# Projections as two 64-row tiles of the array side by side, with kv's sums a chunk later

## The chip, the cores and the metric

The kernel runs on one core of a Trainium2 chip. A core has five engines with queues of their own: TensorE (matmuls, PE in the profile, its weight loads PEld), VectorE (DVE), ScalarE (ACT), GpSimd (POOL) and SyncE (SP), which here only issues DMAs. Matmuls read SBUF and write PSUM, eight banks of 128 partitions by 512 float32; VectorE and ScalarE read PSUM out. The metric is the device time of one execution in microseconds.

## What is computed

Two branches of a block on the same x (2048 x 512), mixed by a gate. All inputs are float32.

```python
def _A_ref(x, wqkv, w_phi, wo):                      # 32 heads of 16
    qkv = (x @ wqkv) ...                             # q, k, v per head
    pq = einsum("bhsd,hdf->bhsf", q, w_phi)
    pk = einsum("bhsd,hdf->bhsf", k, w_phi)
    phi_q = concat([softmax(pq), softmax(-pq)])      # 32 features per head
    phi_k = concat([softmax(pk), softmax(-pk)])
    kv = einsum("bhsf,bhsd->bhfd", phi_k, v)
    z  = einsum("bhsf->bhf", phi_k)
    num = einsum("bhqf,bhfd->bhqd", phi_q, kv)
    den = einsum("bhqf,bhf->bhq", phi_q, z)[..., None] + 1e-6
    return (num / den) ... @ wo
def _B_ref(x, w1, b1, w2):                           # 512 -> 1376 -> 512
    h = x @ w1 + b1
    return (h * tanh(softplus(h))) @ w2
g = sigmoid((x * gate_w).sum(-1, keepdims=True))
out = g * _A_ref(x) + (1 - g) * _B_ref(x)
```

kv and z are sums over all 2048 rows, so every k and v must be there before the first num.

## The kernel before

The matrix products keep float32 accuracy by splitting each operand into a high and a low part in the type float32r, whose matmul is quick: a product is hi x hi + hi x lo + lo x hi. w_phi is multiplied into wk and wq at the start (fuse, L213 and fuse_tiles, L219), so k and q come out of the projection as pk and pq.

The first phase, ("A", c), goes over x in eight chunks of 256 rows (c = 0 to 7), each of two row tiles of 128 (t = 0, 1). For each chunk and row tile there are three projections, k, v and q (proj, L230), each one PSUM tile of 128 x 512 that sums 12 matmuls: 4 slices of the 512 contraction rows (128 each) for each of the three products. The stationary operand is x, 128 rows by the 128 rows of the row tile; the moving one is the weight, 128 x 512. Then, for each row tile:

- k (feat_ops, L250): VectorE takes the maximum and the minimum per head (mx, mn), subtracts (d0, d1; L263 and L265) into a tile E of 128 x 1024 in SBUF, ScalarE takes the exponential (E), VectorE sums per head (S), takes the reciprocal (rS) and scales E (ml, L280). GpSimd adds E to zacc (z, L318). E lives in one of four buffers until the sums of kv have read it.
- v: ScalarE copies it to SBUF (ve).
- q: ScalarE copies it to SBUF (qe) and SyncE stores it to DRAM (st), from where the second phase loads it again (lq).
- kv (L320): 16 small matmuls per row tile add E and v into one PSUM tile that is kept over all chunks.

PSUM is handed out under three tags (L116): a with three buffers, dn with four, kv with one. k and q tiles take a, v tiles take dn (the very first v takes kv). A new tile waits until the readers of the one that had its buffer are done.

The second phase, ("B", b), goes over four blocks of 512 rows. It multiplies x by w1 in 11 slices of 128 columns (up), applies Mish, multiplies by w2 (dn), does for q what was done for k, and combines: num, wo and the gate. x is loaded and split again for it: xbh on ScalarE (XH), xbl on VectorE (XL, L403), which take over the buffers of wk. The weights w1 and w2 are loaded piece by piece and split during the first phase (ldw, wh, wl).

The order of work is written out by hand: strings of step names (FIRST to BLOCK, L39 to L86), which run (L199) reads word by word. Each word calls the function recorded under that name for the chunk; a trailing ' means the chunk before, a trailing + the first block of the second phase (or the next block). All instructions are pinned to this order on their engine, so the strings set the queue of every engine. Before, chunks 1 to 5 use ODD and EVEN in turn, 6 uses NEXT and 7 uses LAST:

```python
ODD = """
    k0 xh mx0 mn0 d00 d10 xl ldx k1 wh0 E0 wl0 ldw0 mx1 mn1 d01 d11 v0 wh1 E1 S0 rS0 ml0 z0 ve0 v1 wl1 ldw1
    S1 rS1 ml1 z1 ve1 q0 qe0 st0 q1 qe1 st1 kv' kv
"""
```

Here k0 is the projection k of row tile 0. The kv sums stand behind every second chunk, for that chunk and the one before; for chunks 6 and 7 they are in LAST.

Of the kernel before, what the change touches and what calls it, by code (L numbers as in the profile page):

```python
# [15 lines left out]
P = 128  # L16
# [20 lines left out]


FIRST = """  # L39
    fq v0 fh0 fh1 fh2 fh3 fl0 fl1 mx0 mn0 d00 d10 fl2 fl3 xh xl ldx ve0 E0 mx1 mn1 d01 d11 v1 ve1 E1  # L40
    S0 rS0 ml0 z0 ldw0 ldw1 S1 rS1 ml1 z1 q0 qe0 st0 q1 qe1 st1
"""
EVEN = """
    k0 xh mx0 mn0 d00 d10 xl ldx k1 wh0 E0 wl0 ldw0 mx1 mn1 d01 d11 v0 wh1 E1 S0 rS0 ml0 z0 ve0 v1 wl1 ldw1
    S1 rS1 ml1 z1 ve1 q0 qe0 st0 q1 qe1 st1
"""
ODD = """
    k0 xh mx0 mn0 d00 d10 xl ldx k1 wh0 E0 wl0 ldw0 mx1 mn1 d01 d11 v0 wh1 E1 S0 rS0 ml0 z0 ve0 v1 wl1 ldw1
    S1 rS1 ml1 z1 ve1 q0 qe0 st0 q1 qe1 st1 kv' kv
"""  # L50
NEXT = """
    lq0+ k0 xh mx0 mn0 d00 d10 xl ldx k1 wh0 E0 wl0 ldw0 mx1 mn1 d01 d11 wh1 E1 S0 rS0 ml0 z0 v0 ve0 wl1 ldw1
    S1 rS1 ml1 z1 v1 ve1 q0 mx0+ mn0+ d00+ d10+ qe0 st0 q1 qe1 st1 E0+ lq1+
"""
LAST = """
    k0 mx0 mn0 d00 d10 k1 E0 XH0 kv' mx1 mn1 d01 d11 E1 v0 S0 rS0 ml0 z0 ve0 ldo XH1 mx1+ mn1+ d01+ d11+ E1+
    S1 rS1 ml1 z1 XL0 XL1 v1 ve1 lq2+ q0 WH0 qe0 st0 q1 WH1 zh qe1 st1 zl kv S0+ rS0+ km
"""

BLOCK0 = """
    up0 mi0 hi0 lo0 gr lq3 S1 rS1 mx2 mn2 d02 d12 up1 @z mi1 hi1 lo1 T0 D0 m0 de0 rd0 sc0 es0 tr0 up2 mi2 hi2 lo2 WL0 dn0
# [7 lines left out]
BLOCK1 = """  # L71
# [7 lines left out]
BLOCK = """  # L79
# [10 lines left out]
def tile_gated_mix(ctx: ExitStack, tc: tile.TileContext, xT, wv, wkT, wqT, bd, w1a, w1b, b1, w2a, w2b, wo, out):  # L90
# [4 lines left out]

    nm = [0]
    pin = tc.keep_in_program_order
    V, G_, A_, Sy = nc.vector, nc.gpsimd, nc.scalar, nc.sync

    def mm(*a, **k):  # L100
        return pin(nc.tensor.matmul(*a, **k))  # L101
# [5 lines left out]
    def k8(name, tag, dt=F32R):  # L107
        return T([P, 2048], dt, tag, 1, name)
# [4 lines left out]
    def k2(name, tag, dt=F32):  # L113
        return T([P, 512], dt, tag, {"pq": 3, "io": 4, "hl": 8}[tag], name)

    def psum(name, tag, bufs={"a": 3, "dn": 4, "kv": 1}):  # L116
        nm[0] += 1
        return pp.tile([P, 512], F32, name=f"{name}_{nm[0]}", tag=tag, bufs=bufs[tag])

    def act(out_, in_, fn=AF.Copy, **k):  # L120
        return pin(A_.activation(out_, in_, fn, **k))  # L121
# [48 lines left out]
    ps = psum("warm", "dn")  # L170
# [35 lines left out]
    wkh, wkl, wvh, wvl, wqh, wql = [
        kt(k8(n, t), 512) for n, t in (("wkh", "xbh"), ("wkl", "xbl"), ("wvh", "woh"), ("wvl", "wol"), ("wqh", "tt"), ("wql", "eT"))]
    xs, Es, vs, psA = {}, {}, {}, {}
# [18 lines left out]
                        mm(acc[r // 64][c : c + 64, o : o + 64], staged[r : r + 64, k, G, c : c + 64], bds[r : r + 64, G, r : r + 64], start=True, stop=True, skip_group_check=True)  # L227
        return acc

    def proj(x, t, wh, wl, tag):  # L230
        ps = psum("proj", tag)
        xh, xl = x
        sl = slice(t * P, (t + 1) * P)
        n = 0
        for a, w in ((xh, wh), (xh, wl), (xl, wh)):
            for k in range(KT):
                mm(ps, a[k // 2][:, k % 2, sl], w[:, k, :], start=(n == 0), stop=(n == 3 * KT - 1))
                n += 1
        return ps
# [10 lines left out]
    def feat_ops(key, t, src, d):  # L250

        n = str(t)

        def red(name, op):
            d[name] = T([P, H], F32, name, 2, name)
            pin(V.tensor_reduce(d[name], hv(src()), axis=AX.X, op=op))  # L256

        def dd(a):
            if "E" not in d:
                d["E"] = k4("E", "E")  # L260
            E = hv(d["E"][:, a * 512 : (a + 1) * 512])
            if a == 0:
                pin(V.tensor_sub(E, hv(src()), d["mx"][:, :, None].to_broadcast([P, H, DH])))  # L263
            else:
                pin(V.tensor_sub(E, d["mn"][:, :, None].to_broadcast([P, H, DH]), hv(src())))  # L265

        def ss():
            d["S"] = T([P, 2 * H], F32, "Sm", 2, "Sm")
            pin(V.tensor_reduce(d["S"], hv(d["E"][:, :]), axis=AX.X, op=ALU.add))  # L269
# [12 lines left out]
    def a_ops(c):  # L282
        key = ("A", c)
        P_ = psA[c] = {}
        for t in range(2):
            d = {}
            Es[c, t] = d

            def k_(t=t):
                P_["k", t] = proj(xs[c], t, wkh, wkl, "a")  # L290

            def v_(t=t):
                P_["v", t] = proj(xs[c], t, wvh, wvl, "dn" if c or t else "kv")

            def q_(t=t):
                P_["q", t] = proj(xs[c], t, wqh, wql, "a")
# [12 lines left out]

            at(key, f"k{t}", k_)  # L310
            at(key, f"v{t}", v_)
            at(key, f"q{t}", q_)
            at(key, f"ve{t}", ve)
            at(key, f"qe{t}", qe)
            at(key, f"st{t}", st)
            feat_ops(key, t, lambda t=t: P_["k", t][:, :], d)
            at(key, f"ml{t}", lambda d=d: scale_by(d, V))
            at(key, f"z{t}", lambda d=d: pin(G_.tensor_add(zacc, zacc, d["E"])))  # L318

        def kv():  # L320
# [115 lines left out]
    B = {}  # L436
# [266 lines left out]

    for t in range(2):
        psA[0]["k", t] = pk[t]
        del steps[("A", 0), f"k{t}"]

    run(FIRST, ("A", 0))
    for c in range(1, NCH):
        run((EVEN, ODD)[c % 2] if c < NCH - 2 else NEXT if c < NCH - 1 else LAST, ("A", c), ("A", c - 1), ("B", 0))  # L710
    for b in range(NB):
        run((BLOCK0, BLOCK1, BLOCK, BLOCK)[b], ("B", b), ("B", b - 1), ("B", b + 1))
    assert not steps, list(steps)


# [58 lines left out]
```

## Time and profile before

| | us |
|---|---|
| median of 3 runs | 457.28 (456.52 to 458.05) |
| span of the profiled execution | 455.6 |
| TensorE busy | 445.6 |
| VectorE busy | 306.8 |
| ScalarE busy | 195.0 |
| GpSimd busy | 161.4 |

The span is that of one execution from its first to its last instruction, taken by the hardware profiler; what the runs take beyond it is 1.7 us by the median. In rows of the profile, "L101 PE MATMUL proj<-wkh,xh 128\*128 128x512" is a matmul recorded at line 101 (a helper that all matmuls go through), which writes proj from wkh and xh, with a tile of the array of 128 rows by 128 columns and an output of 128 x 512. The number after x is how many; then come busy microseconds and the mean length of one in ns. Matmuls overlap in the pipeline, so the time from one start to the next, not the length of one, is what a matmul costs. "[1.51 <-DVE xbl L403]" is idle time before an instruction and what ended it. SBUF and PSUM types of four bytes are both shown as f32.

### The profile page before, as it was taken

Reading aid. Unit: us, or ns where it says so; the run is one execution under the profiler, and the core shown is the slowest. Engines: PE = TensorE matmul, PEld = TensorE weight load, DVE = VectorE, ACT = ScalarE, POOL = GpSimd, SP = SyncE. Lnnn points to the kernel's source line nnn. Section 1 sums busy time; section 2 is a strip of 40 time slices with the busy share of each in tenths; the row PEclk is TensorE's granted clock in tenths of the full one; section 3 lists DMA queues with packets and bytes.
Section 4 is the critical chain, followed back from the end, with each engine's and each line's share of the span. In section 5 each row is a group of like instructions: output and inputs, shape, how many; then the busy total and the mean of one; then the engine's idle time right before and its main releaser. Section 6 shows DMA issues by size and latency. Waiting matters only on the chain.

```text
span 455.6 us, 6980 instructions
## 1 busy us (share of the span) xinstructions
PE 445.6 (98%) x2772; PEld 363.4 (80%) x2772; DVE 306.8 (67%) x402; ACT 195.0 (43%) x265; POOL 161.4 (35%) x102
## 2 busy tenths in 40 slices
PE   7999999999999899999899999999999999999996
PEld 6888888888888678878687887887887888787885
DVE  2599459369399999799987985666967629611002
ACT  3554443443334645726337354434254553234220
POOL 3338777767862355221123212023212122221211
PEclk9999999999999999999999999999999999999999
DMA  7721513505523110313434050332041402030002
GB/s 284 247 83 56 168 53 129 186 8 179 183 82 106 47 23 2 94 46 86 146 94 138 17 158 14 108 115 54 23 119 53 112 19 94 1 81 13 1 1 92
DMA packets 25593, 40.07 MB, mean 88 GB/s; under 512 B 5716, under 2 KB 13908, under 8 KB 25560
## 3 DMA queue, kind: packets, MB, share of 16 engines
q1 hardware_dynamic: 25384, 39.35, 28.4%
q8 instruction: 22, 0.36, 0.3%
q10 hardware_dynamic: 144, 0.26, 0.2%
q14 instruction: 11, 0.09, 0.1%
q0 software_dynamic: 32, 0.01, 0.0%
HBM read 22.82 MB, written 8.40 MB: 69 GB/s over the span
## 4 chain that ended last, share of the span: by engine, by line
PE 61%; DVE 4%; ACT 1%; issue 0%
PE up L101 25%; PE down L101 24%; PE wo L101 10%; PE num L101 2%; DVE xbl L403 1%; DVE Sm L269 1%; DVE T L548 0%; DVE Dn L552 0%; DVE io L633 0%; ACT L121 0%; DVE tt L566 0%; DVE E L280 0%; DVE Dn L572 0%; ACT E L121 0%; DVE Sm L277 0%; ACT io L121 0%
## 5 line engine op out<-in xcount | busy, mean ns | idle before, releaser
L498 POOL TENSOR_TENSOR l<-act,h 128x512 fp32r<-128x512 f32 x44 | 60.7, 1380 | 224.2 <-ACT h L121 189.4
L121 ACT ACTIVATE act<-up,b1s 128x512 f32<-128x512 f32 x44 | 30.3, 689 | 91.5 <-PE up L101 90.3
L318 POOL TENSOR_TENSOR zacc<-zacc,E 128x1024 f32<-128x1024 f32 x16 | 39.7, 2482 | 45.8 <-DVE E L280 31.4
L121 ACT ACTIVATE E<-E 128x1024 f32<-128x1024 f32 x32 | 33.6, 1059 | 49.4 <-DVE E L265 49.4
L280 DVE TENSOR_TENSOR E<-E,Sm 128x1024 f32<-128x1024 f32 x32 | 44.0, 1375 | 1.1
L101 PE MATMUL wo<-woh,ohl 128*128 128x512 f32 x128 | 40.8, 390 | 1.2 <-DVE ohl L607 1.2
L269 DVE TENSOR_REDUCE Sm<-E 128x64 f32<-128x1024 f32 x32 | 38.7, 1209 | 3.8 <-ACT E L121 3.8
L101 PE MATMUL down<-w2ah,h 128*128 128x512 f32 x96 | 37.5, 390 | 0.0
L101 PE MATMUL down<-w2al,h 128*128 128x512 f32 x96 | 37.4, 389 | 0.0
L101 PE MATMUL down<-w2ah,l 128*128 128x512 f32 x96 | 37.4, 389 | 0.0
L633 DVE SCALAR_TENSOR_TENSOR io<-down,og_sb,io 128x512 f32<-128x512 f32 x16 | 11.3, 751 | 31.1 <-PE down L101 31.0
L256 DVE TENSOR_REDUCE mx<-proj 128x32 f32<-128x512 f32 x16 | 11.0, 689 | 30.8 <-PE proj L101 30.8
L101 PE MATMUL down<-w2bh,h 128*128 128x512 f32 x80 | 31.2, 391 | 0.0
L101 PE MATMUL down<-w2bl,h 128*128 128x512 f32 x80 | 31.1, 389 | 0.0
L101 PE MATMUL down<-w2bh,l 128*128 128x512 f32 x80 | 31.1, 389 | 0.0
L101 PEld LDWEIGHTS wo<-woh,ohl 128*128 128x128 f32 x128 | 24.0, 188 | 6.6 <-DVE ohl L607 1.6
L121 ACT ACT_TABLE_LOAD x19 | 24.4, 1283 | 10.1 <-PE up L101 9.8
L121 ACT ACTIVATE h<-act 128x512 fp32r<-128x512 f32 x44 | 27.8, 632 | 1.4
L607 DVE TENSOR_TENSOR ohl<-num,ohl 128x512 fp32r<-128x512 f32 x16 | 10.2, 678 | 26.4 <-ACT ohl L121 26.4
L101 PE MATMUL up<-xbl,w1ah 128*128 128x512 f32 x96 | 25.8, 391 | 1.5 <-DVE xbl L403 1.5
L101 PE MATMUL up<-xbh,w1ah 128*128 128x512 f32 x96 | 26.3, 396 | 0.2 <-ACT zb L121 0.2
L101 PE MATMUL up<-xbh,w1al 128*128 128x512 f32 x96 | 25.7, 389 | 0.0
(113 smaller groups left out, 970.6 us busy)
## 6 DMA issues: line engine op xcount, KB each, us to landing
xraw<-in_xT_dram SPq DMA_DIRECT2D x16, 512.0 KB, 4.8
eT<-tt SPq DMA_DIRECT2D x128, 64.0 KB, 2.0
pqd<-qs SPq DMA_DIRECT2D x16, 256.0 KB, 3.5
pq<-pqd SPq DMA_DIRECT2D x16, 256.0 KB, 2.8
out_dram<-io SPq DMA_DIRECT2D x16, 256.0 KB, 2.1
raw<-in_w1a_dram SPq DMA_DIRECT2D x3, 512.0 KB, 3.6
raw<-in_w2a_dram SPq DMA_DIRECT2D x3, 512.0 KB, 3.7
wT<-in_wkT_dram SPq DMA_DIRECT2D x4, 256.0 KB, 5.4
```

The source lines that it names most:

```text
L101: return pin(nc.tensor.matmul(*a, **k))
L121: return pin(A_.activation(out_, in_, fn, **k))
L256: pin(V.tensor_reduce(d[name], hv(src()), axis=AX.X, op=op))
L269: pin(V.tensor_reduce(d["S"], hv(d["E"][:, :]), axis=AX.X, op=ALU.add))
L280: pin(eng.tensor_mul(hv(d["E"][:, :]), hv(d["E"][:, :]), d["S"][:, :, None].to_broadcast([P, 2 * H, DH])))
L318: at(key, f"z{t}", lambda d=d: pin(G_.tensor_add(zacc, zacc, d["E"])))
L403: pin(V.tensor_sub(xb[b][1][:, :, sl], kt(raw[h], SC), f32(xb[b][0][:, :, sl])))
L498: pin(G_.tensor_sub(U[i]["l"], U[i]["a"], f32(U[i]["h"])))
L607: pin(V.tensor_sub(ohl[h, gp][:, 512:], num[h, gp], f32(ohl[h, gp][:, :512])))
L633: pin(V.scalar_tensor_tensor(io[t], dn[t], og_sb[:, i : i + 1], io[t], op0=ALU.mult, op1=ALU.add))
```

## The change

proj becomes proj2, which makes both row tiles of a chunk together. Each slice of 128 contraction rows is cut in two of 64, and each matmul is a tile of 64 x 128 of the array: rows 0 to 63 in its upper half, rows 64 to 127 in its lower half. In the first half of a projection (turn 0) the upper tile adds rows 0 to 63 into row tile 0 and the lower tile rows 64 to 127 into row tile 1; in the second half (turn 1) it is the other way round. So the two tiles write different PSUM banks at all times. Each half has 24 matmuls in 12 pairs. Between the halves stands a dependency: a SyncE step waits for the last matmul of the first half, and the first matmul of the second half waits for that step.

The words k1, v1, q1 now mean the first half of both row tiles, k2, v2, q2 the second half; after it both row tiles are there at once. In the strings another projection (or more) stands between the two halves. The kv sums run between v1 and k2 of every second chunk, for the two chunks before it (kv" and kv'), in LAST for chunk 6 behind k2, and for chunk 7 behind up0 of BLOCK0, with km. In chunk 0, k is computed as before (k_part, L661).

```diff
 FIRST = """
-    fq v0 fh0 ... ldx ve0 E0 mx1 mn1 d01 d11 v1 ve1 E1
-    S0 rS0 ml0 z0 ldw0 ldw1 S1 rS1 ml1 z1 q0 qe0 st0 q1 qe1 st1
+    fq v1 fh0 fh1 fh2 fh3 fl0 fl1 mx0 mn0 d00 d10 fl2 fl3 xh xl ldx q1 v2 ve0 E0 mx1 mn1 d01 d11 ve1 E1
+    S0 rS0 ml0 z0 ldw0 ldw1 S1 rS1 ml1 z1 q2 qe0 st0 qe1 st1
 """
...
+FRONT = """
+    k1 v1 kv" kv' k2 xh mx0 mn0 d00 d10 xl q1 ldx wh0 E0 wl0 ldw0 mx1 mn1 d01 d11 v2 wh1 E1 S0 rS0 ml0 z0 ve0 ve1
+    q2 wl1 ldw1 S1 rS1 ml1 z1 qe0 st0 qe1 st1
 """
+BACK = FRONT.replace("""kv" kv'""", "")
...
 LAST = """
+    k1 v1 k2 mx0 mn0 d00 d10 E0 XH0 kv' q1 mx1 mn1 d01 d11 E1 v2 S0 rS0 ml0 z0 ve0 ve1 ldo XH1
+    S1 rS1 ml1 z1 mx1+ mn1+ d01+ d11+ E1+ XL0 XL1 lq2+ q2 WH0 qe0 st0 WH1 zh qe1 st1 zl S0+ rS0+
 """
 BLOCK0 = """
-    up0 mi0 hi0 lo0 gr lq3 S1 rS1 ...
+    up0 mi0 hi0 lo0 gr kv' km' lq3 S1 rS1 ...
...
-    def proj(x, t, wh, wl, tag):
...
+    def proj2(x, wh, wl, tags):
+        ps = [psum("proj", tag) for tag in tags]
         xh, xl = x
+        ops = [(a[k // 2][:, k % 2, :], w[:, k, :]) for a, w in ((xh, wh), (xh, wl), (xl, wh)) for k in range(KT)]
+        done = []
+
+        def turn(n):
+            for i, (a, w) in enumerate(ops):
+                for j, r in enumerate((0, 64)):
+                    t = j ^ n
+                    ins = mm(ps[t], a[r : r + 64, t * P : (t + 1) * P], w[r : r + 64, :], start=(n == 0 and i == 0), stop=(n == 1 and i == len(ops) - 1), skip_group_check=True)
+                    if n and not i and not j:
+                        tc.add_manual_dep(ins.ins, done[0].ins.name, SYNC, reason="the sums change over")
+            if not n:
+                done.append(pin(Sy.nop()))
+                tc.add_manual_dep(done[0].ins, ins.ins.name, SYNC, reason="the first halves are summed")
+
+        return ps, turn
...
+        if c:
+            both("k", wkh, wkl, "aa")
+        both("v", wvh, wvl, ("dn" if c else "kv", "dn"))
+        both("q", wqh, wql, "aa")
...
-        run((EVEN, ODD)[c % 2] if c < NCH - 2 else NEXT if c < NCH - 1 else LAST, ...)
+        run((FRONT, BACK)[c % 2] if c < NCH - 2 else NEXT if c < NCH - 1 else LAST, ...)
```

The function both records turn 0 under the name with 1 (there the two PSUM tiles are taken) and turn 1 under the name with 2. NEXT (chunk 6) has the order of FRONT with the first steps of the second phase put in; run understands a trailing " as two chunks back. The readers of the projections, feat_ops, ve, qe and st, are as before, one per row tile.

More of the change, by code (lines that the diff above doesn't have):

```diff
@@ L39 @@
 FIRST = """
-    fq v0 fh0 fh1 fh2 fh3 fl0 fl1 mx0 mn0 d00 d10 fl2 fl3 xh xl ldx ve0 E0 mx1 mn1 d01 d11 v1 ve1 E1
-    S0 rS0 ml0 z0 ldw0 ldw1 S1 rS1 ml1 z1 q0 qe0 st0 q1 qe1 st1
-"""
-EVEN = """
-    k0 xh mx0 mn0 d00 d10 xl ldx k1 wh0 E0 wl0 ldw0 mx1 mn1 d01 d11 v0 wh1 E1 S0 rS0 ml0 z0 ve0 v1 wl1 ldw1
-    S1 rS1 ml1 z1 ve1 q0 qe0 st0 q1 qe1 st1
-"""
[L47 to L50, printed above, removed]
+    fq v1 fh0 fh1 fh2 fh3 fl0 fl1 mx0 mn0 d00 d10 fl2 fl3 xh xl ldx q1 v2 ve0 E0 mx1 mn1 d01 d11 ve1 E1
+    S0 rS0 ml0 z0 ldw0 ldw1 S1 rS1 ml1 z1 q2 qe0 st0 qe1 st1
+"""
+FRONT = """
+    k1 v1 kv" kv' k2 xh mx0 mn0 d00 d10 xl q1 ldx wh0 E0 wl0 ldw0 mx1 mn1 d01 d11 v2 wh1 E1 S0 rS0 ml0 z0 ve0 ve1
+    q2 wl1 ldw1 S1 rS1 ml1 z1 qe0 st0 qe1 st1
+"""
+BACK = FRONT.replace("""kv" kv'""", "")
 NEXT = """
-    lq0+ k0 xh mx0 mn0 d00 d10 xl ldx k1 wh0 E0 wl0 ldw0 mx1 mn1 d01 d11 wh1 E1 S0 rS0 ml0 z0 v0 ve0 wl1 ldw1
-    S1 rS1 ml1 z1 v1 ve1 q0 mx0+ mn0+ d00+ d10+ qe0 st0 q1 qe1 st1 E0+ lq1+
+    lq0+ k1 v1 kv" kv' k2 xh mx0 mn0 d00 d10 xl q1 ldx wh0 E0 wl0 ldw0 mx1 mn1 d01 d11 v2 wh1 E1 S0 rS0 ml0 z0 ve0 ve1
+    q2 wl1 ldw1 S1 rS1 ml1 z1 mx0+ mn0+ d00+ d10+ qe0 st0 qe1 st1 E0+ lq1+
 """
 LAST = """
-    k0 mx0 mn0 d00 d10 k1 E0 XH0 kv' mx1 mn1 d01 d11 E1 v0 S0 rS0 ml0 z0 ve0 ldo XH1 mx1+ mn1+ d01+ d11+ E1+
-    S1 rS1 ml1 z1 XL0 XL1 v1 ve1 lq2+ q0 WH0 qe0 st0 q1 WH1 zh qe1 st1 zl kv S0+ rS0+ km
+    k1 v1 k2 mx0 mn0 d00 d10 E0 XH0 kv' q1 mx1 mn1 d01 d11 E1 v2 S0 rS0 ml0 z0 ve0 ve1 ldo XH1
+    S1 rS1 ml1 z1 mx1+ mn1+ d01+ d11+ E1+ XL0 XL1 lq2+ q2 WH0 qe0 st0 WH1 zh qe1 st1 zl S0+ rS0+
 """
 BLOCK0 = """
-    up0 mi0 hi0 lo0 gr lq3 S1 rS1 mx2 mn2 d02 d12 up1 @z mi1 hi1 lo1 T0 D0 m0 de0 rd0 sc0 es0 tr0 up2 mi2 hi2 lo2 WL0 dn0
+    up0 mi0 hi0 lo0 gr kv' km' lq3 S1 rS1 mx2 mn2 d02 d12 up1 @z mi1 hi1 lo1 T0 D0 m0 de0 rd0 sc0 es0 tr0 up2 mi2 hi2 lo2 WL0 dn0
     T1 D1 m1 de1 rd1 sc1 es1 tr1 mv0 lq0+ lq1+ mx3 mn3 d03 d13 up3 @kt mi3 hi3 lo3 WL1 dn1
@@ L97, in tile_gated_mix @@
     pin = tc.keep_in_program_order
+    SYNC = mybir.DependencyInfo(mybir.DependencyClass.Sync, mybir.DependencyReason.DATA)
     V, G_, A_, Sy = nc.vector, nc.gpsimd, nc.scalar, nc.sync
@@ L200, in run @@
         for w in text.split():
-            k = prev if w.endswith("'") else nxt if w.endswith("+") else key
-            for fn in steps.pop((k, w.rstrip("'+")), ()):
+            k = (key[0], key[1] - 2) if w.endswith('"') else prev if w.endswith("'") else nxt if w.endswith("+") else key
+            for fn in steps.pop((k, w.rstrip("'+\"")), ()):
                 fn()
@@ L228, in fuse_tiles @@
         return acc
-    def proj(x, t, wh, wl, tag):
-        ps = psum("proj", tag)
+    def proj2(x, wh, wl, tags):
+        ps = [psum("proj", tag) for tag in tags]
         xh, xl = x
[L233 to L239, printed above, removed]
+        ops = [(a[k // 2][:, k % 2, :], w[:, k, :]) for a, w in ((xh, wh), (xh, wl), (xl, wh)) for k in range(KT)]
[11 more added lines that the diff above has]
+        return ps, turn
     def new_x(c):
@@ L284, in a_ops, with both, one @@
         P_ = psA[c] = {}
+        def both(n, wh, wl, tags):
+            turns = []
+            def one():
+                ps, turn = proj2(xs[c], wh, wl, tags)
+                P_[n, 0], P_[n, 1] = ps
+                turn(0)
+                turns.append(turn)
+            at(key, n + "1", one)
+            at(key, n + "2", lambda: turns[0](1))
+        if c:
+            both("k", wkh, wkl, "aa")
+        both("v", wvh, wvl, ("dn" if c else "kv", "dn"))
+        both("q", wqh, wql, "aa")
         for t in range(2):
@@ L287, in a_ops @@
             Es[c, t] = d
[L289 to L296, printed above, removed]
             def ve(t=t):
@@ L308, in st @@
                 pin(Sy.dma_start(pqd[i * P : (i + 1) * P, :], P_["qs", t]))
-            at(key, f"k{t}", k_)
-            at(key, f"v{t}", v_)
-            at(key, f"q{t}", q_)
             at(key, f"ve{t}", ve)
@@ L705, in tile_gated_mix @@
         psA[0]["k", t] = pk[t]
-        del steps[("A", 0), f"k{t}"]
     run(FIRST, ("A", 0))
     for c in range(1, NCH):
-        run((EVEN, ODD)[c % 2] if c < NCH - 2 else NEXT if c < NCH - 1 else LAST, ("A", c), ("A", c - 1), ("B", 0))
+        run((FRONT, BACK)[c % 2] if c < NCH - 2 else NEXT if c < NCH - 1 else LAST, ("A", c), ("A", c - 1), ("B", 0))
     for b in range(NB):
-        run((BLOCK0, BLOCK1, BLOCK, BLOCK)[b], ("B", b), ("B", b - 1), ("B", b + 1))
+        run((BLOCK0, BLOCK1, BLOCK, BLOCK)[b], ("B", b), ("B", b - 1) if b else ("A", NCH - 1), ("B", b + 1))
     assert not steps, list(steps)
```

## The prediction

> **What bounds the kernel now.** I read the page first: the busy shares, the clock row and the chain that ended last.
>
> ```profile
> span 455.6 us, 6980 instructions
> ...
> PE 445.6 (98%) x2772; PEld 363.4 (80%) x2772; DVE 306.8 (67%) x402; ACT 195.0 (43%) x265; POOL 161.4 (35%) x102
> ...
> PEclk9999999999999999999999999999999999999999
> ...
> PE 61%; DVE 4%; ACT 1%; issue 0%
> ```
>
> TensorE is busy all through and its clock is granted throughout, so the time is what TensorE executes plus the few moments at which it waits. Next come those waits, in the view of who waited for whom, and the table by stretch for one chunk of the projection phase (the columns of the second are the length, then each engine's busy time, the granted clock and the DMA share).
>
> ```profile
> PE fuse L101 <- DMA bds<-in_bd_dram: 2.1, 1, 2.1
> PE up L101 <- DVE xbl L403: 1.5, 1, 1.5
> ```
>
> ```profile
> 48.60:66.50 17.90, 17.90 (x87) 14.82 (x80) 11.44 (x14) 6.76 (x10) 12.46 (x7) 1.00 0.38 116
> ```
>
> The one wait that the change will touch stands in the timelines of TensorE and of VectorE, at the end of the projections (start, length, engine, instructions):
>
> ```profile
> 152.31 1.10 PE L101 MATMUL kvp<-E,v 128*32 128x64 f32 x64
> 153.34 1.20 PE L101 MATMUL up<-xbh,w1ah 128*128 128x512 f32 x4
> 154.37 1.07 PE L101 MATMUL up<-xbh,w1al 128*128 128x512 f32 x4
> 156.95 1.20 PE L101 MATMUL up<-xbl,w1ah 128*128 128x512 f32 x4 [1.51 <-DVE xbl L403]
> ```
>
> ```profile
> 152.35 4.55 DVE L403 TENSOR_TENSOR xbl<-xraw,xbh 128x1024 fp32r<-128x1024 f32 x2
> ```
>
> Two things are read off for later: a chunk's kv sums take 153.34 - 152.31 = 1.03 us, and TensorE goes on 0.05 us after VectorE's end (156.90, then 156.95).
>
> In a chunk TensorE has no gap, while VectorE works 11.4 of 17.9 us. So in this phase a microsecond in which TensorE stands still is a microsecond of the whole kernel, and VectorE has slack.
>
> **The unit price of a projection matmul**, from the timeline of TensorE (rows of four matmuls) and the groups by form, first and last of the nine groups of 64 that the projections make:
>
> ```profile
> 50.56 1.07 PE L101 MATMUL proj<-wkh,xl 128*128 128x512 f32 x4
> ...
> 61.44 1.07 PE L101 MATMUL proj<-wqh,xl 128*128 128x512 f32 x4
> 62.35 1.07 PE L101 MATMUL proj<-wqh,xh 128*128 128x512 f32 x4
> ```
>
> ```profile
> L101 PE MATMUL proj<-wkh,xh 128*128 128x512 f32 x64 | 18.7, 398 | 0.0
> ...
> L101 PE MATMUL proj<-wqh,xl 128*128 128x512 f32 x64 | 17.1, 389 | 0.0
> ```
>
> Four take 62.35 - 61.44 = 0.91 us, so one matmul takes 0.227 us. Nine groups of 64 are 576; the 24 of chunk 0's k (issued piecewise while the weights are fused) stay as they are. The change turns the other 552 into 552 pairs of matmuls with 64 contraction rows, one pair member in the upper, one in the lower half of the array.
>
> **Price of a pair.** No 64x128 tile stands in this trace. The nearest rows are the other tiled groups and an untiled one in plain float32:
>
> ```profile
> 12.13 1.05 PE L101 MATMUL fuse<-bds,wT 128*128 128x128 f32 x8
> ...
> 17.24 2.10 PE L101 MATMUL fuse<-bds,wT 64*64 64x64 f32 x128
> 19.27 0.50 PE L101 MATMUL proj<-wvh,xh 128*128 128x512 f32 x1
> ...
> 218.40 1.09 PE L101 MATMUL num<-eT,kvb 64*32 64x256 f32 x32
> ```
>
> The first row: (1.05 - 0.28)/7 = 0.11 us for 128 float32 columns, twice the price per column of the float32r projections (0.227 for 512). The last row is 32 matmuls in four rounds of eight tiles: its length less one matmul (0.38) and the seven issues inside a round (0.05), over three rounds, is 0.22 us per round, just what 256 float32 columns cost alone at 0.11 per 128. So the eight tiles, two row halves among them, run at the same time. The second row says the same: 32 rounds of four in 1.9 us are 0.06 each, the 64 columns of one. A pair then costs no more than the 512 columns that it streams: from 0.216 (a num round at its best, by the same count) to 0.227 (the untiled matmul). I take 0.218, nearest to num, whose form it shares. Gain: 552 x (0.227 - 0.218) = 5 us; the ends are 6 and 0. That is all that the tiles themselves can bring, since the same columns still stream.
>
> **The new wait on PSUM, q after k.** The pool tag a has three buffers (L116). Before, k0, k1, q0, q1 took them in turn, and each was read out while another projection ran. Now a chunk's k pair takes two at once and its q pair needs the third and the first again. In the changed order q1 (the first half of q) stands directly behind k2, and its second matmul waits for VectorE's second subtraction on k's row tile 0, which can begin only when k2 has ended. All of TensorE stands behind that matmul. What is late follows from chunk 2, VectorE's and ScalarE's timelines:
>
> ```profile
> 51.67 0.69 DVE L256 TENSOR_REDUCE mx<-proj 128x32 f32<-128x512 f32 x1 [6.55 <-PE proj L101]
> 52.28 0.68 DVE L256 TENSOR_REDUCE mn<-proj 128x32 f32<-128x512 f32 x1
> 52.88 0.68 DVE L263 TENSOR_TENSOR E<-proj,mx 128x512 f32<-128x512 f32 x1
> 53.47 0.68 DVE L265 TENSOR_TENSOR E<-mn,proj 128x512 f32<-128x512 f32 x1
> ```
>
> ```profile
> 62.60 0.60 ACT L121 ACTIVATE qs<-proj 128x512 f32<-128x512 f32 x1 [2.17 <-PE proj L101]
> ```
>
> The last matmul of k0 there starts at 50.56 + 3 x 0.227 = 51.24; VectorE begins 0.43 later and needs 54.15 - 51.67 = 2.48 us for the four operations. With the 0.05 us back to TensorE, q1 goes on 2.97 us after k2's last start instead of 0.22: 2.75 us lost. VectorE is free at that time: its 11.4 us on a chunk end some 12 us after k2, and the next k2 comes about 20 us after it. Six chunks (1 to 6) lose 2.75; in chunk 7 the kv sums of chunk 6 stand between (kv' behind k2) (0.1 us of changeover and 1.03) and leave 1.6. Sum 18.1 us, within 0.5 either way.
>
> **The second wait, k after q.** The next chunk's k1 takes the buffer of the q pair's row tile 0, just finished by q2. ScalarE's copy: last q start 62.12, copy 62.60 to 63.20, 1.13 us after it with the way back instead of 0.22; 0.91 lost. Seven times (chunks 1 to 7): 6.4 us, 6.0 to 6.6.
>
> **First chunk.** VectorE's timeline there:
>
> ```profile
> 19.06 1.29 DVE L702 TENSOR_TENSOR wql<-fuse,wqh 128x512 fp32r<-128x512 f32 x2 [3.04 <-ACT wqh L121]
> ...
> 22.06 0.68 DVE L265 TENSOR_TENSOR E<-mn,proj 128x512 f32<-128x512 f32 x1
> ```
>
> v1 now opens two PSUM tiles at once, and the second is freed by the first of the two wql subtractions (about 19.75, where v starts at 19.27): 0.45 late. q1 needs chunk 0's k buffer, free at 22.74, while v1 ends near 22.35: 0.45 more. Together 1 us, 0.6 to 1.2.
>
> **Entry into the second phase.** up0 needs the split of x (xbl), last in VectorE's list of chunk 7:
>
> ```profile
> 140.28 0.69 DVE L256 TENSOR_REDUCE mx<-proj 128x32 f32<-128x512 f32 x1 [0.23 <-PE proj L101]
> ...
> 142.68 1.21 DVE L269 TENSOR_REDUCE Sm<-E 128x64 f32<-128x1024 f32 x1
> ...
> 145.66 0.68 DVE L256 TENSOR_REDUCE mx<-pq 128x32 f32<-128x512 f32 x1
> ...
> 149.38 1.21 DVE L269 TENSOR_REDUCE Sm<-E 128x64 f32<-128x1024 f32 x1
> ```
>
> Now both row tiles of k arrive only at the end of k2. From there VectorE needs 0.43, row tile 0's four operations (2.4) and the list above from 140.28 to 156.9 (16.6): 19.4 us. Part of that is VectorE slowed beside GpSimd: xbl took 2.3 each here, the scaling 1.23 or 1.89; without it the list is 2.4 + 3.0 + 2.4 + 3.0 + 2.4 = 13.2, the end at 16.0. TensorE reaches the third quarter of up0 at 2.97 + 36 x 0.218 + 0.1 + 8 x 0.227 = 12.7. It waits 3.3 to 6.7, against 156.95 - 155.28 = 1.67 lost before: 1.6 to 5.0 more, and I take 3.5.
>
> **At nothing.** The sums of kv move one chunk but number the same, in five visits as before. Their inputs are ready: VectorE's last scaling of the chunk before ends about 12 us after that chunk's k2, and kv comes at 2.97 + 3 x 2.6 (q1, v2, q2) + 0.9 + 2 x 2.6 (k1, v1) = 16.9. The 23 SyncE steps that tell a second half that the first halves are summed have a whole projection (2.6 us) in which to do so; without that cover each would cost what VectorE's start costs above, about 0.43. On SyncE's queue the loads of the next x and weights stand behind such a step (the one of q1), ScalarE's splits wait for them, and for those k1 of the next chunk. A load takes
>
> ```profile
> xraw<-in_xT_dram SPq DMA_DIRECT2D x16, 512.0 KB, 4.8
> ```
>
> 4.8 us and is asked for a chunk ahead, some 20 us, so a start later by one projection stays hidden.
>
> **Sum**: 18.1 + 6.4 + 1.0 + 3.5 - 5.0 = +24 us. The profiled execution goes from 455.6 to 479.6; the median of the runs shown is 457.28, 1.7 above that span, so 481.3. The low ends together give +20.3 (477.6), the high ends +31.3 (488.6).
>
> **Rivals.**
> First, the clock. It starts low, as the timeline shows:
>
> ```profile
> 6.17 4.75 PE L101 MATMUL fuse<-bds,wT 128*128 128x128 f32 x24 [2.12 <-DMA bds<-in_bd_dram]
> ```
>
> 24 matmuls that cost 0.11 each later (2.7 us) took 4.75: 2.1 us lost after an idle start. Should each of the eight long waits (seven behind k2, one at xbl) lower it again, that is 8 x 2.1 = 17 us on top, 498. Against it: the 2.1 us wait for bds and the 1.5 us one for xbl leave the clock row at 9. Chance 7%. At the xbl wait alone, the longest, it is 2 us, 483: I hold that possible, one time in three within the forecast, and the range has it. The Trainium skill (TensorE: Matmul & The Clock Gate, section "HAM oscillation — how this bites in real kernels") puts the limit at an idle gap over about 3.4 us; by that the waits of 2.75 would keep the clock and the xbl wait might lose it. This trace has no such gap and can't say.
>
> Second, the pair members run one after the other: 552 x 0.227 = 125 us more, with the waits about 612. For it: num and fuse stream float32 at half the rate, so two full-rate streams into two PSUM banks are not shown. Against: eight tiles share a round at no cost. Chance 4%.
>
> Third, not slower: a 64-row tile streams its columns faster than a 128-row one. It decides when the pair saves what the waits cost, 29 us over 552, or 0.053: a pair at 0.174 or less gives 457. At 0.16 it would be 449. Against it stand the num and fuse rounds, which cost their columns in full. Chance 3%; 2% for just about even.
>
> **How the numbers follow.** Forecast 84%, clock 7%, serial 4%, not slower 5%. A kernel of this length tells 0.3% (1.4 us) from no change. Faster 0.03, same 0.02, slower 0.95. The range 475 to 491 takes the bounds of the sum, with 2 us of clock at the top and 2.5 at the bottom for VectorE's four operations being nearer than I make them.
>
> **What would show it.** Right: TensorE idles about 2.5 us seven times before proj<-wqh, released by VectorE's E of L265 (its new line), and about 0.8 us seven times before proj<-wkh, released by ScalarE's qs; one wait for xbl of 3 to 7 us; 64-row starts in pairs some 0.22 apart. Wrong: pairs 0.45 apart (serial), a clock row under 9 in the first third, or no idle time behind k2, which would mean that the buffers don't turn as I read them.

## The result and the profile after

| | before | after |
|---|---|---|
| median, us | 457.07 (456.52 to 458.05) | 495.76 (495.61 to 496.1) |
| span of the profiled execution, us | 455.6 | 493.9 |

The ratio is 1.0839 (95% interval 1.0821 to 1.0858): 38.7 us slower, where 24 were forecast, and above the range. The page after, its totals and its clock row:

```profile
PE 458.5 (93%) x3324; PEld 376.5 (76%) x3324; DVE 306.1 (62%) x402; ACT 193.8 (39%) x265; POOL 160.9 (33%) x102
...
PEclk9998989998998997999999999999999999999999
```

TensorE is now idle for 35.4 us (493.9 - 458.5), against 10.0 before, so about 25 of the 38 us are waiting. The other 13 are in its busy time, although the same columns stream: 458.5 against 445.6. The clock row says where to look: five of the first 16 slices read 8 or 7, where before there were only nines; the mean granted clock is 0.978 against 0.998. First the waits, by who waited for whom (total, times, longest):

```profile
PE proj L99 <- DVE E L273: 16.5, 7, 2.7
PE proj L99 <- ACT qs L119: 4.9, 7, 0.8
PE up L99 <- DVE xbl L416: 4.4, 1, 4.4
```

These are the three waits of the forecast, in its order and number. The view counts idle time, and a matmul's modelled end lies after the next one's start, so the time lost between starts is a little more. It is read from TensorE's timeline, here at chunk 1:

```profile
29.66 0.39 PE L99 MATMUL proj<-wkh,xh 64*128 64x512 f32 x1
30.82 1.21 PE L99 MATMUL proj<-wkh,xh 64*128 64x512 f32 x7 [0.77 <-ACT qs L119]
...
36.21 1.29 PE L99 MATMUL proj<-wkh,xh 64*128 64x512 f32 x8
37.12 1.29 PE L99 MATMUL proj<-wkl,xh 64*128 64x512 f32 x8
...
38.93 0.39 PE L99 MATMUL proj<-wqh,xh 64*128 64x512 f32 x1
41.98 1.81 PE L99 MATMUL proj<-wqh,xh 64*128 64x512 f32 x7 [2.66 <-DVE E L273]
43.23 2.27 PE L99 MATMUL proj<-wql,xh 64*128 64x512 f32 x8
44.94 1.61 PE L99 MATMUL proj<-wqh,xl 64*128 64x512 f32 x8
```

Eight matmuls, four pairs, take 37.12 - 36.21 = 0.907 us: 0.2267 a pair, exactly the price of one untiled matmul. The single matmul at 38.93 is the first of q1; its partner waits until 41.98, which is 3.05 - 0.23 = 2.82 us lost. Then comes what the forecast did not have: from 43.23 four pairs take 44.94 - 43.23 = 1.71 us, nearly twice the price. The table by stretch, cut at the moments at which the trace's clock records change, shows why (columns: stretch, length, busy time of PE, PEld, DVE, ACT and POOL with their counts, granted clock, DMA share, GB/s):

```profile
38.83:42.24 3.41, 0.75 (x8) 0.36 (x6) 2.89 (x5) 0.38 (x1) 3.41 (x3) 1.00 0.00 0
42.24:45.65 3.41, 3.41 (x18) 3.13 (x18) 3.38 (x6) 2.69 (x3) 0.70 (x1) 0.50 0.00 0
...
127.55:130.96 3.41, 1.97 (x18) 1.31 (x14) 1.41 (x3) 0.00 (x0) 1.07 (x1) 1.00 0.00 0
130.96:134.37 3.41, 2.19 (x20) 2.11 (x22) 3.41 (x7) 2.01 (x2) 0.00 (x0) 1.00 0.00 0
134.37:137.78 3.41, 3.41 (x34) 3.22 (x32) 3.34 (x5) 1.06 (x1) 0.21 (x1) 1.00 0.46 132
...
185.60:189.01 3.41, 1.38 (x6) 0.77 (x5) 3.41 (x5) 0.00 (x0) 2.33 (x1) 1.00 0.01 4
189.01:195.84 6.83, 4.43 (x69) 3.36 (x70) 4.60 (x5) 6.64 (x8) 0.00 (x0) 0.50 0.20 77
```

After a stretch in which TensorE was busy for only 0.75 of 3.41 us, the granted clock is 0.50 for the next 3.41 us: 18 matmuls where the stretch from 134.37 has 34. The half-speed stretches start at 42.24, 66.13, 110.5 and 154.88 (chunks 1, 2, 4, 6; 3.41 us each) and at 189.01 (6.83 us, behind the wait for xbl). All of these moments lie a whole number of 3.41 us apart, so the clock is set in windows of a fixed grid. Chunk 5 shows the other case. Its wait is as long as that of chunk 1, but it falls across a boundary of the grid:

```profile
129.13 0.39 PE L99 MATMUL proj<-wqh,xh 64*128 64x512 f32 x1
132.18 1.16 PE L99 MATMUL proj<-wqh,xh 64*128 64x512 f32 x7 [2.66 <-DVE E L273]
```

By starts TensorE stands still for 1.63 us of one window and 1.19 of the next (by the table it is busy 1.97 and 2.19), and the clock stays at 1.00. One half-speed window costs 1.7 us; the long one, less 2.4 us in which TensorE still waited, 2.2: together 4 x 1.7 + 2.2 = 9.0 us.

So by starts, the span's 38.3 us are: 17.8 behind k2 (2.82, 2.60, 2.83, 2.60, 2.82, 2.61, 1.48), 6.0 before k1, 0.8 in the first chunk, 2.9 more at xbl, 9.0 of clock, 0.9 at the kv visits (below), less 1.3 because the first v starts at 18.00 where it started at 19.27 (the reason stands below, with the clock). That makes 36.1. Another 1.5 us are in the same halves: behind a stop the matmuls take a little longer until they run as before. An undisturbed half lasts 2.72 us (38.93 - 36.21); the seven halves of k1 last 7.1 us longer than that, and the seven of q1 25.0, of which 6.8 are clock, so the two waits cost 18.2 and 7.1 in all. Most of the last 0.7 us is lost behind the first z of the second phase and is not assigned.

### The profile page after: what moved, and what is told of

The parts are those of the page before. It is cut to its first block, busy times and chain, and to the rows that moved or that the text cites. A ratio compares the mean times of both kernels' runs of the same rounds, so it can differ in the third digit from the quotient of the medians.

```text
span 493.9 us, 8101 instructions
## 1 busy us (share of the span) xinstructions
PE 458.5 (93%) x3324; PEld 376.5 (76%) x3324; DVE 306.1 (62%) x402; ACT 193.8 (39%) x265; POOL 160.9 (33%) x102
## 4 chain that ended last, share of the span: by engine, by line
PE 57%; DVE 3%; ACT 1%; issue 0%
PE up L99 23%; PE down L99 22%; PE wo L99 9%; PE num L99 1%; DVE Sm L277 0%; DVE xbl L416 0%; DVE T L561 0%; DVE Dn L565 0%; DVE io L646 0%; PE kvp L99 0%; ACT L119 0%; DVE tt L579 0%; DVE E L288 0%; DVE Dn L585 0%; ACT E L119 0%; DVE Sm L285 0%
## 5 line engine op out<-in xcount | busy, mean ns | idle before, releaser
L511 POOL TENSOR_TENSOR l<-act,h 128x512 fp32r<-128x512 f32 x44 | 62.3, 1415 | 229.2 <-ACT h L119 194.3
L288 DVE TENSOR_TENSOR E<-E,Sm 128x1024 f32<-128x1024 f32 x32 | 47.7, 1490 | 1.1
L277 DVE TENSOR_REDUCE Sm<-E 128x64 f32<-128x1024 f32 x32 | 38.7, 1210 | 7.7 <-ACT E L119 7.7
L99 PE MATMUL proj<-wqh,xh 64*128 64x512 f32 x128 | 25.3, 444 | 16.5 <-DVE E L273 16.5
L99 PEld LDWEIGHTS proj<-wqh,xh 64*128 64x128 f32 x128 | 16.8, 200 | 20.6 <-issue 19.2
L119 ACT ACT_TABLE_LOAD x19 | 24.4, 1283 | 10.1 <-PE up L99 9.8
L99 PE MATMUL proj<-wkh,xh 64*128 64x512 f32 (+1 forms) x120 | 23.1, 408 | 4.9 <-ACT qs L119 4.9
```

Source lines behind the costliest of these rows:

```text
L511: pin(G_.tensor_sub(U[i]["l"], U[i]["a"], f32(U[i]["h"])))
```

## The experiments

Each changes the kernel after, unless it says otherwise. The timings are medians; each ratio is to runs of the kernel before that were made beside it, with medians of 456.93 to 457.73.

**What the two PSUM waits cost.** Tag dn has four buffers, of which v's pair uses two.

```diff
-        both("q", wqh, wql, "aa")
+        both("q", wqh, wql, ("dn", "dn") if c else "aa")
```

> The q pair of chunks 1 to 7 takes its two PSUM tiles from the tag dn instead of a; nothing else changes. Theory (the 39 us are waits for PSUM buffers, 27 us, and the half-speed clock that follows idle TensorE, 10 us; a pair costs what an untiled matmul costs, 0.227): no wait behind k2 and none behind q2, no half-speed stretch in the first phase, pairs still 0.227 apart; only the wait for xbl stays and grows to about 6.7 us, since TensorE arrives earlier, with 3.4 us of clock loss: about 467 us. Rival 1 (the tiles themselves lower the clock): waits go, half-speed stretches stay, about 474. Rival 2 (the SyncE step between the halves is what TensorE waits for): waits stay, about 495.

Measured: 476.89 us, ratio 1.0428 (1.0396 to 1.0461). Both waits are gone (qs stands once, behind the first chunk) and 18.9 us with them, but the time is 10 us above what I expected. TensorE's waits and its timeline in chunk 3:

```profile
PE proj L99 <- SPq L244: 6.7, 4, 2.9
PE up L99 <- DVE xbl L416: 6.1, 1, 6.1
```

```profile
74.28 1.19 PE L99 MATMUL proj<-wkh,xh 64*128 64x512 f32 x8 [1.61 <-SPq L244]
```

A new wait took the place of the old ones: k2 waits for the SyncE step that says that k1 is summed. On SyncE's timeline the load behind which the step stands, and on GpSimd's what that load waits for:

```profile
62.34 10.88 SPq L157 DMA_DIRECT2D raw<-in_w1b_dram  x2
```

```profile
69.50 3.37 POOL L383 TENSOR_TENSOR w1bl<-raw,w1bh 128x1024 fp32r<-128x1024 f32 x1
```

SyncE sits on the load of the next weights until GpSimd has split the last ones (69.50 + 3.37 = 72.87); two stores follow (0.86 us), then the step, and k2 at 74.28. In the kernel after, the same load holds SyncE until 77.44, but there TensorE ends k1 only at 79.4, so the step comes in time for k2 at 82.12.

**The step on another queue.**

```diff
-                done.append(pin(Sy.nop()))
+                done.append(pin(eng.nop()))        # ScalarE for c > 0, SyncE in chunk 0
```

> As e1_q_in_dn, and the step between the halves stands on ScalarE's queue instead of SyncE's for chunks 1 to 7. In e1 TensorE waited four times (6.7 us) for that step before k2, and SyncE held it up because the load of a weight piece ahead of it waited for GpSimd's split. Theory (queue order on SyncE): these waits vanish (7.4 us with latency) and the half-speed stretch behind the longest of them (1.7 us); the wait for xbl stays at 6 us: 466 to 468 us. Rival (the dependency itself costs, whichever engine carries it): waits before k2 stay, now put down to ScalarE, 474 to 477.

Measured: 469.21 us, ratio 1.0273 (1.0248 to 1.0299); 7.7 less than with the step on SyncE, and 1 us above what I expected. Of it 4.0 us are the step's waits (6.7 before, 2.7 now) and 2.2 are clock: a half-speed window of 3.41 us at 150.7 is gone (1.7), and behind xbl TensorE works 5.1 us at half speed where it was 6.2 (0.5). The rest is not assigned. The four SyncE waits are gone; one wait is left, because ScalarE has a queue too. In chunk 7 the step stands behind the exponential E0+, which waits for VectorE (ScalarE's and TensorE's timelines):

```profile
144.53 1.06 ACT L119 ACTIVATE E<-E 128x1024 f32<-128x1024 f32 x1 [6.91 <-DVE E L273]
```

```profile
144.63 1.20 PE L99 MATMUL proj<-wkh,xh 64*128 64x512 f32 x8 [2.74 <-ACTq L244]
```

**The clock by itself: the same wait, but with a busy array.** While q1's second matmul waits, the first one is repeated 11 times (its sum starts anew each time, so the result is the same).

```diff
+                    if fill and not n and not i and j:
+                        for _ in range(fill):
+                            mm(ps[0], ops[0][0][0:64, 0:P], ops[0][1][0:64, :], start=True, stop=False, skip_group_check=True)
```

> In chunks 1 to 7 the first matmul of q is issued eleven times more, into the row tile whose buffer is free, before the matmul that waits; its sum starts anew each time, so only the last counts. Theory (the clock falls because TensorE idles): q goes on at the same time after k2 as before, but the four half-speed stretches behind k2 are gone, 1.7 us each, the double one at xbl stays: 489 us. Rival 1 (the clock falls because of the tiles): 495 or more, the stretches stay.

Measured: 489.55 us, ratio 1.071 (1.068 to 1.0741). The clock row and chunk 1 on TensorE's timeline:

```profile
PEclk9999999999999998999999999999999999999999
```

```profile
40.34 2.88 PE L100 MATMUL proj<-wqh,xh 64*128 64x512 f32 x12
43.38 1.17 PE L100 MATMUL proj<-wqh,xh 64*128 64x512 f32 x7 [0.17 <-DVE E L277]
44.18 1.28 PE L100 MATMUL proj<-wql,xh 64*128 64x512 f32 x8
```

q1 goes on 3.04 us after its start, as in the kernel after (3.05), but what follows runs at full speed. Four windows of 1.7 us are 6.8; 6.2 were gained. So the clock fell because TensorE stood still, not because of the tiles: the time behind k2 is lost in both kernels, and the clock is lost on top of it.

**How much idle time halves the clock.** The same with 4 repeats.

> As e2_fill11 with four repeats instead of eleven: idle behind k2 falls from 2.5-2.7 us to about 1.6-1.8. In the changed kernel the half-speed windows (3.41 us long, on a fixed grid) followed exactly those waits of which 1.9 us or more fell into one window of the grid. If the limit lies between 1.6 and 1.9 us idle in a window, about half of it, there are no half-speed windows behind k2: 489 us as with eleven. If any wait over 1.5 us can do it, some stay: 491 to 494.

Measured: 497.25 us, ratio 1.0858 (1.0836 to 1.0879): none of the half-speed windows went, neither what I expected of a limit near 1.6 to 1.9 us nor of a higher one. The table by stretch for chunk 1:

```profile
39.71:43.12 3.41, 1.65 (x12) 1.12 (x10) 3.02 (x6) 0.51 (x1) 3.41 (x3) 1.00 0.00 0
43.12:46.53 3.41, 3.41 (x20) 3.10 (x18) 3.38 (x6) 2.55 (x3) 0.62 (x1) 0.50 0.00 0
```

By starts TensorE stood still for 1.91, 1.70, 1.70 and 1.70 us in the four windows that were followed by half speed. That would put the limit just above the 1.63 us of chunk 5, but two other traces speak against it. With 11 repeats the wait for xbl leaves 1.99 us of standing still in one window (182.68 to 184.67), and the next stays at 1.00; the drop comes a window later. With q in dn a window with 1.77 us (72.51 to 74.28) is not followed by half speed either:

```profile
181.25:184.67 3.42, 1.59 (x7) 0.95 (x6) 3.42 (x4) 0.43 (x1) 1.75 (x1) 1.00 0.00 0
184.67:188.08 3.41, 1.60 (x38) 1.16 (x42) 1.75 (x2) 3.41 (x5) 0.00 (x0) 1.00 0.14 55
```

```profile
72.19:75.60 3.41, 1.80 (x18) 1.16 (x16) 0.00 (x0) 0.00 (x0) 3.41 (x3) 1.00 0.45 138
75.60:79.01 3.41, 3.41 (x34) 2.80 (x32) 1.65 (x3) 0.00 (x0) 3.41 (x3) 1.00 0.24 93
```

So no single length of idle time fits all traces. In the windows with 4 repeats, five matmuls run with one 64-row tile alone; whether such a matmul counts for less than a pair was not tested. Over all traces, behind the first 12 us, a window at full clock with 2.2 us or more of standing still was always followed by half speed, and one with 1.63 us or less never was. This kernel is 1.5 us slower than the one after, but not in the projections: from the first v to up0 it takes 166.81 us, and the one after 166.86. About 0.75 is lost ahead of the first v (18.75 against 18.00) and 0.5 behind the first z.

**kv's sums behind k2 instead of ahead of it**, so that they cover a part of the wait in every second chunk.

```diff
-    k1 v1 kv" kv' k2 xh ...
+    k1 v1 k2 kv" kv' xh ...
```

> The kv sums of chunks 2, 4 and 6 stand behind k2 instead of before it; nothing else changes. Theory (the wait behind k2 is the 2.5 us of VectorE's four operations, whatever TensorE does meanwhile): idle time behind k2 in these three chunks falls from 2.45 to about 0.5, kv costs nothing there, and their half-speed stretches go: 3 x (1.95 + 1.7) = 11 us, 485 us. Rival 2 (the SyncE step): no change, 495.

Measured: 486.27 us, ratio 1.0643 (1.0613 to 1.0673), 9.5 less than after. The wait behind k2 falls from 16.5 to 10.1 us in total, and its rest is too short for the clock in the chunks with kv (TensorE's timeline, chunk 2):

```profile
61.77 1.99 PE L99 MATMUL kvp<-E,v 128*32 128x64 f32 x128
63.69 0.50 PE L99 MATMUL proj<-wqh,xh 64*128 64x512 f32 x1
64.50 1.16 PE L99 MATMUL proj<-wqh,xh 64*128 64x512 f32 x7 [0.31 <-DVE E L273]
```

6.4 us of waiting and two of the four windows (3.4) make 9.8.

**The order without the tiles.** proj2 with whole matmuls: turn 1 is row tile 0, turn 2 row tile 1.

```diff
-                for j, r in enumerate((0, 64)):
-                    t = j ^ n
-                    ins = mm(ps[t], a[r : r + 64, t * P : (t + 1) * P], w[r : r + 64, :], ...)
...
+                mm(ps[n], a[:, n * P : (n + 1) * P], w, start=(i == 0), stop=(i == len(ops) - 1))
```

> Everything of the change stays (order, kv's place, PSUM tiles taken in pairs) but the tiles: the first half is row tile 0 whole, the second row tile 1 whole, with 128 contraction rows each, and no SyncE step. Theory: the waits come from both row tiles being ready only at the end; so none behind k2 or q2, kv's later place costs nothing, and what is left is a longer wait for xbl (about 4.4 instead of 1.5 us, with up to 3.4 us of clock): 460 to 463 us. Rival 3 (the late kv or the order itself costs much): over 470.

Measured: 461.27 us, ratio 1.0099 (1.0065 to 1.0133). No wait behind k2 or q2 is left. The 4.2 us above before are at xbl: 4.0 us idle there against 1.5, and one half-speed window behind it (1.7). The order and kv's later place as such cost no more; the 34 us between this kernel and the one after come with the pair of tiles: both row tiles are complete only at the end of the second half, and a step stands between the halves.

**What a projection matmul costs beyond its columns.** The kernel before, each projection matmul cut into two of 256 columns.

```diff
-                mm(ps, a[k // 2][:, k % 2, sl], w[:, k, :], start=(n == 0), stop=(n == 3 * KT - 1))
-                n += 1
+                ops.append((a[k // 2][:, k % 2, sl], w[:, k, :]))
+        for o in (0, 256):
+            for n, (a, w) in enumerate(ops):
+                mm(ps[:, o : o + 256], a, w[:, o : o + 256], start=(n == 0), stop=(n == 3 * KT - 1))
```

> The kernel before, with every projection matmul of chunks 0 to 7 but chunk 0's k cut into two of 256 columns (all 12 for the left half of the bank, then all 12 for the right): 552 matmuls become 1104. It prices the 0.227 us of a 512-column float32r matmul, against 0.216 for a round of num. If the excess of 0.011 is a fixed cost of each matmul, starts are 0.120 apart and the kernel takes 4 to 7 us more (462 to 464); if it goes with the columns streamed, starts are 0.113 apart and the time is that of before. Then no tile shape can win it back, and the pairs had nothing to gain.

Measured: 463.66 us (one run), 6.6 above the 457.07 of before. TensorE's timeline:

```profile
51.42 0.64 PE L101 MATMUL proj<-wkh,xh 128*128 128x256 f32 x4
51.90 0.64 PE L101 MATMUL proj<-wkl,xh 128*128 128x256 f32 x4
```

0.48 / 4 = 0.120 us for 256 columns, 0.2267 for 512: 0.1067 us per 256 columns and a fixed 0.0133 per float32r matmul; 552 of these are 7.3 us. A pair took 0.2267, so both its members pay the fixed part at once, and a pair of half the rows costs what the whole matmul did. The 5 us of gain were meant to come out of this fixed part.

**The wait at xbl.** Three runs asked whether it can be taken away by moving xbl's two subtractions ahead of the second phase's first steps (mx1+ to E1+) in VectorE's order. On the kernel with q in dn and the step on ScalarE:

```diff
-    S1 rS1 ml1 z1 mx1+ mn1+ d01+ d11+ E1+ XL0 XL1 lq2+ q2 ...
+    S1 rS1 ml1 z1 XL0 XL1 mx1+ mn1+ d01+ d11+ E1+ lq2+ q2 ...
```

> As e5, and in LAST the split of x for the second phase (XL0, XL1) stands ahead of the second phase's first four operations (mx1+ to d11+) on VectorE. Theory (what is left of the loss is the xbl wait, which is VectorE's list): the wait falls by 2.4 to 3.9 us to 2 to 4 us, with fewer half-speed windows: 461 to 464 us, and never under before, since a pair costs what an untiled matmul costs. Rival (the tiles do gain, 5 us, hidden so far): 458 or less.

Measured: 472.69 us, ratio 1.0343 (1.0318 to 1.0367): a miss, 3.5 us slower than without the move. The wait for xbl falls from 6.1 to 4.3 us, but at the second phase's first z there are new waits of 2.0 us for ScalarE's gr and 0.6 for VectorE's zs, and the trace has two half-speed windows more (at 145.95 and 176.67). And the same move in the kernel before:

> The kernel before, with XL0 and XL1 ahead of mx1+ mn1+ d01+ d11+ E1+ in LAST. Theory (the one wait for xbl of before, 1.5 us, is VectorE's list too): it goes away or nearly, the first wo or zb may take a little back: 455.3 to 456.5 us, ratio 0.996 to 0.999. Rival: the wait moves to zb or to the second phase's features, no change.

Measured: 463.23 us, ratio 1.0138 (1.0117 to 1.016), also a miss. TensorE's last kv sums waited 5.0 us for the copy of v, and ScalarE's timeline shows what was overlooked:

```profile
157.28 1.06 ACT L121 ACTIVATE E<-E 128x1024 f32<-128x1024 f32 x1 [10.54 <-DVE E L265]
158.24 0.58 ACT L121 ACTIVATE v<-proj 128x512 f32<-128x512 f32 x1
```

E1+, ScalarE's exponential, now waits 10.54 us for the later VectorE steps, and behind it on ScalarE stands the copy of v that the last kv sums read. TensorE waits for that. So E1+ has to move too, behind qe1 st1:

```diff
-    S1 rS1 ml1 z1 XL0 XL1 mx1+ mn1+ d01+ d11+ E1+ v1 ve1 lq2+ q0 WH0 qe0 st0 q1 WH1 zh qe1 st1 zl ...
+    S1 rS1 ml1 z1 XL0 XL1 mx1+ mn1+ d01+ d11+ v1 ve1 lq2+ q0 WH0 qe0 st0 q1 WH1 zh qe1 st1 E1+ zl ...
```

> As e8 (the kernel before with XL0 and XL1 first on VectorE), but E1+ stands at the end of ScalarE's list of chunk 7 instead of ahead of ve1. In e8 TensorE waited 5.0 us in kv for ScalarE's copy of v, which stood behind E1+. Theory (e8 lost to that queue order, not to the earlier XL): no wait in kv and none for xbl, 455.5 to 457 us, at or slightly under before. Rival (VectorE's list is simply too long there, and the wait comes back elsewhere by zs or S1): 458 or more.

Measured: 456.62 us over 12 runs (455.92 to 458.0), ratio 0.9979 (0.9965 to 0.9993). The wait for xbl is gone, and TensorE goes through up0 without a stop; the exponential that is now late takes more than half of it back (TensorE's waits; ScalarE's gr stands behind E1+ in its queue):

```profile
PE z L101 <- ACT gr L121: 1.2, 1, 1.2
```

It is the only version below the kernel before, by 0.2%: the interval leaves 1 out, but the gain is under the 0.3% that the forecast took as telling a change from none.

**All at once.** The kernel after with q in dn, the step on ScalarE, xbl first, E1+ late and E0+ in LAST behind E0.

> The tiled pairs with q in dn and the step on ScalarE (e5), XL0 and XL1 first on VectorE, E0+ moved into chunk 7 (in e5 it held ScalarE, and with it the step, for 2.7 us) and E1+ to the end of ScalarE's list. Theory (pairs at 0.227 gain nothing, so with the waits gone the kernel comes back to before plus what the first chunk and the rest of the xbl wait cost): waits 0.8 (qs, once) and 2 to 5 for xbl, with up to 3.4 us of clock: 459 to 464 us. Rival (pairs gain 5 us): under 457.

Measured: 464.98 us, ratio 1.0151 (1.0136 to 1.0165), just above what I expected; a pair that saved 5 us would have given under 457. The longest wait that is left on TensorE, and the price of its pairs:

```profile
PE up L99 <- DVE xbl L416: 4.6, 1, 4.6
```

```profile
60.86 1.07 PE L99 MATMUL proj<-wqh,xl 64*128 64x512 f32 x8
61.77 1.07 PE L99 MATMUL proj<-wvh,xh 64*128 64x512 f32 x8
```

0.907 us for four pairs again. VectorE is late for xbl although xbl comes first: it starts on k's row tile 0 at 145.15, works without a pause until xbl ends at 161.07, and TensorE is at up0 from 154.45. The profiled execution is 7.0 us above that of before (462.6 and 455.6): 3.1 more at xbl, 1.5 of clock behind it, 1.1 before chunk 1's k1 (the wait for qs), 0.6 more in chunk 0, and 0.2 at the kv sums of chunk 2; 0.5 is not assigned.

## Why the prediction was wrong, step by step

**The bound** was right: in the projection phase what TensorE loses is lost by the kernel. With the waits behind k2 and q2 taken away, the time fell by 18.9 us, and by 7.7 more when SyncE's waits went too.

**q after k**, 18.1 us forecast, 17.8 measured, in the forecast's number and place, with chunk 7 shorter (1.48 against 1.6).

**k after q**, 6.4 forecast, 6.0 measured.

**First chunk**, 1.0 forecast, 0.8 measured.

**xbl**, 3.5 forecast, 2.9 measured.

**The pair price was mis-sized.** The forecast took 0.218 from num; the pair costs 0.2267, the upper end. Gain 0 instead of 5. The count by which the tiles run at the same time was right (the rival of serial pairs fell), but num was the wrong neighbour: it is plain float32, and what a float32r matmul pays beyond its columns (0.0133 us, by the matmuls of 256 columns) is paid by a pair as by one.

**The clock is the step that failed.** The forecast gave it 7%, "Against it: the 2.1 us wait for bds and the 1.5 us one for xbl leave the clock row at 9", and within the forecast itself counted it once, at xbl. It cost 9.0 us after five waits; 11 repeated matmuls that change nothing but the idle time took 6.2 of them away. The sign that the forecast named for itself, a clock row under 9 in the first third, is what the row after shows. The quoted reason was no evidence. The wait for xbl was 1.67 us by starts, less than any of the waits behind k2 in chunks 1 to 6 (2.60 to 2.83). And the wait for bds ends at 6.17, ahead of the trace's first clock record, which is at 9.97; the clock row counts the time before that as full speed, but TensorE ran at half speed there. Of the 24 fuse matmuls that start at 6.17 the last six are

```profile
9.96 0.84 PE L101 MATMUL fuse<-bds,wT 128*128 128x128 f32 x6
```

so 18 start within 3.79 us, 0.21 each, and these six 0.11 apart, with the change at the first clock record. In the trace of the kernel after, where the first record is at 4.69, the same matmuls are 0.11 apart:

```profile
5.61 2.05 PE L99 MATMUL fuse<-bds,wT 128*128 128x128 f32 x16 [1.56 <-DMA bds<-in_bd_dram]
```

So the rival's 2.1 us was mostly a price of the clock, but of the slow start and not of a wait; a wait cost 1.7 where it cost any. Of the 1.3 us by which the first v comes earlier after the change, 0.6 are bds's earlier landing (fuse starts at 5.61, not 6.17), and 0.7 this clock less a new wait for wT. The change touches nothing ahead of the first v, and the first clock record lies anywhere from 4.36 to 12.10 us in the thirteen traces, so I count these 1.3 us as luck.

The Trainium skill's limit (TensorE: Matmul & The Clock Gate, section "HAM oscillation — how this bites in real kernels"), an idle gap of some 3.4 us, does not hold here: 2.60 us inside one window were enough in chunks 2, 4 and 6. Of the rival's eight waits, the one of chunk 7 was short (1.48 us), and for the others it decided where they fell on the grid: two were split over two windows (chunks 3 and 5) and cost no clock, five did.

**kv at nothing** was right for the sums themselves. In chunk 2 the last matmul of v1 starts at 58.06, the first of kv at 58.38 and k2 at 60.30:

```profile
58.06 0.39 PE L99 MATMUL proj<-wvh,xl 64*128 64x512 f32 x1
58.38 1.99 PE L99 MATMUL kvp<-E,v 128*32 128x64 f32 x128
60.30 1.20 PE L99 MATMUL proj<-wkh,xh 64*128 64x512 f32 x8
```

From the last projection matmul to the next are 2.24 us, as at the same visit between untiled projections before (46.38 to 48.62). What each visit adds, 0.22 us, comes from the late partner: since the wait at k1 the two row tiles are one matmul out of step, so the last matmul ahead of kv runs alone and takes the time of a pair. Four such visits are 0.9 us. In the last experiment, where the tiles are in step from chunk 2's kv on, the visits of chunks 4 and 6 add nothing.

**The SyncE steps at nothing** held only under cover. Without it 0.43 us each was forecast. The wait is not that of the signal but of SyncE's queue: 6.7 us, as soon as the PSUM waits no longer held TensorE back longer.

The sum with the measured terms: 479.6 + 5 for the pairs + 9 for the clock = 493.6, and the span is 493.9; the small differences of the other terms and the early start (together -2.8) cancel the kv visits, the slow restarts and what is not assigned (together +3.1). The sum's low end was added wrongly: its terms give +19.8, not +20.3, which moves nothing here.

## What to carry to other kernels

Cutting a full contraction into two row tiles side by side streams the same columns, so it can gain at most the fixed part of a matmul, and here not even that, while two results that open and close together need twice the PSUM and leave no matmuls between a projection's end and its readers. When a change adds a wait to TensorE, price the clock as well as the wait: here a wait of 2.6 to 2.8 us inside one window of the clock's grid cost another 1.7. An instruction that is moved or added on a queue takes the lateness of everything ahead of it there and passes it on to everything behind it, so look at both on every engine, SyncE too, before costing it at nothing.

## What was new of the hardware

- The granted clock changes on a fixed grid of 3.41 us. A window in which TensorE stood still for 2.2 us or more was followed by one at 0.50; 2.82 us of idle time split over two windows (1.63 and 1.19) cost nothing beyond itself. The limit between is not settled: 1.99 us were not followed by half speed with 11 repeats, 1.70 were with 4.
- Ahead of the trace's first clock record (9.97 us before, 4.69 after) the clock row shows full speed, while the 128-column matmuls started 0.21 us apart, against 0.11 from the record on.
- A float32r matmul costs a fixed 0.0133 us beside 0.1067 per 256 columns (0.120 and 0.227 measured), and a pair of 64-row tiles pays it once. When a wait holds one member back, the two tiles stay one matmul out of step, and the last matmul before a change of tiles takes the time of a pair alone (0.22 us).
